# Conversions of the weights w_a and w_b issued behind the gating of the preceding slice, on ACT and on DVE

## Chip, cores, metric

The kernel runs on one core of a Trainium2 chip. The metric is device time in microseconds (us) of one execution; smaller is better. Engines: PE multiplies matrices (PEld is its load of the stationary operand), DVE is the vector engine, ACT the scalar engine, POOL is nearly unused, and SP issues the DMAs. Every engine works through its own instructions in the order in which they were issued to it.

## What is computed

Three stages, each on the output of the one before, on 2304 tokens (4 batches of 512 local and 32 global tokens) of 512 features:

```python
# attention: every local token sees the 32 global keys and a window of 32 keys to either side;
# every global token sees all keys. 8 heads of 64 features.
x = attention(q_l, k_l, v_l, q_g, k_g, v_g)          # (2304, 512)

# first MLP, 512 -> 2048 -> 512
h = x @ w_in
g = np.where(h >= 1, h, np.where(h <= -1, 0.0, (h + 1) ** 2 / 4))
x = g @ w_out

# second MLP, 512 -> 1536 -> 512
a = x @ w_a
b = x @ w_b
out = (a * b) @ w_out2                                # float32
```

The weights arrive as 64-bit floats.

## The kernel before

**Tiles and slices.** The tokens are cut into six tiles (`TILES`, line 43): tiles 0 to 4 have three blocks of 128 tokens, tile 5 one block and the global tokens. The first MLP walks the tiles, and in each tile the 16 slices of 128 hidden features. A pair (t, f) is a unit of the loop at line 728. A unit calls `h_unit(t, f)` (x times w_in, 12 matmuls into a PSUM tile hp), and then `x_unit` of the unit two before (`LAG` at line 727): the gated slice times w_out, 12 matmuls into four PSUM accumulators acc. Every product is three matmuls (`mm3`, lines 423 to 425), since each operand is split into a high and a low part in fp32r.

**The gating** of a slice follows its hp matmuls: ACT takes a relu (line 696), DVE two steps (lines 697 and 698). Its last two instructions, the split of the result g into high and low (ACT line 701, DVE line 702), are put off to the next unit by `flush`.

**Attention** of tile t + 1 runs between the units of tile t (lines 795 to 799). `att_atoms` yields it in pieces per block and pair of heads: load q and k (line 154, two buffers), cast them on ACT (166, 167) and take the rest on DVE (168, 169), score matmuls s (179, 180), masked minimum on DVE (199), exponentials on ACT (203), normalisation (207 to 210), transposes tp on PE (216), copy pt on ACT (220), product with v (226), copy out on DVE (230). The PSUM tiles hp, s, tp and o share four buffers with the tag "h". When a tile begins, its attention output is split into xh on ACT (405) and xl on DVE (406). The global rows, kg and vg (lines 254 and 259), are done in tile 4.

**Conversions.** A weight slice comes as 128 x 512 numbers of 64 bits (`w_load`, one DMA of 512 KB on SP, two raw buffers from tile 1 on). `w_conv` makes 32-bit floats of it: one instruction on ACT, three on DVE:

```python
 97        nc.scalar.activation(tf, f32(high), AF.Copy, scale=W_DOWN)
 98        nc.vector.tensor_scalar(t, t, 3, 0x7FFFFFFF, ALU.logical_shift_left, ALU.bitwise_and)
 99        nc.vector.scalar_tensor_tensor(t, high, -0x80000000, t, ALU.bitwise_and, ALU.bitwise_or)
100        nc.vector.scalar_tensor_tensor(t, low, 29, t, ALU.logical_shift_right, ALU.bitwise_or)
```

In tile 0 the weights of the first MLP are converted as it goes. The 24 slices of w_a and w_b are converted during tiles 1 to 3, ahead of every second unit, and parked in DRAM (wd) until the second MLP loads them again, from the end of tile 4 on:

```python
742                if 1 <= t <= 3 and f % 2 == 0:
743                    i = 8 * (t - 1) + f // 2
744                    if i == 0:
745                        w_load(*ab2[0])
746                    if i + 1 < len(ab2):
747                        w_load(*ab2[i + 1])
748                    (nm, f2), tf = w_conv()
749                    nc.sync.dma_start(wd[f2]["ab".index(nm)], tf)
```

**What sets the order.** The code above is a trace, not the order of issue. A scheduler goes through it with a model of the engines: of the instructions whose operands and buffers are ready it takes the one that was traced first, engine by engine. So an instruction may be issued well ahead of its place in the code, when its engine is idle in the model and it waits for nothing. A conversion needs its raw weights, one of two raw buffers and one of two result buffers, and nothing of the slice at which it stands.

Of the kernel before, what the change touches and what calls it, by code (L numbers as in the profile page):

```python
# [14 lines left out]
AF = mybir.ActivationFunctionType  # L15
ALU = mybir.AluOpType
# [23 lines left out]
W_UP = 256.0  # L40
# [18 lines left out]
def body(tc, qk, qkd, vw, kg, vg, w1i, w1o, w2a, w2b, w2o, mask, out):  # L59
    nc = tc.nc  # L60
# [11 lines left out]
    half = cp.tile([P, 1], F32, name="half")  # L72
# [4 lines left out]
    def f32(t):  # L77
        return t.bitcast(F32)
# [8 lines left out]
    def w_load(key, src):  # L87
        raw = sp["p"].tile([P, 512, 2], I32, name="wraw", bufs=sp["raw"])
        nc.sync.dma_start(raw, src.bitcast(I32).rearrange("p (f two) -> p f two", two=2))
        wq.append((key, raw))  # L90

    def w_conv():
        key, raw = wq.pop(0)
        low, high = raw[:, :, 0], raw[:, :, 1]
        t = sp["p"].tile([P, 512], I32, name="wt", bufs=sp["wt"])
        tf = f32(t)
        nc.scalar.activation(tf, f32(high), AF.Copy, scale=W_DOWN)
        nc.vector.tensor_scalar(t, t, 3, 0x7FFFFFFF, ALU.logical_shift_left, ALU.bitwise_and)
        nc.vector.scalar_tensor_tensor(t, high, -0x80000000, t, ALU.bitwise_and, ALU.bitwise_or)
        nc.vector.scalar_tensor_tensor(t, low, 29, t, ALU.logical_shift_right, ALU.bitwise_or)  # L100
        return key, tf
# [295 lines left out]
    def x_split(t, W):  # L397
        hi, lo = [], []
        last = t == len(TILES) - 1
        for c in range(NC):  # L400
            pool = x5p if last else mp
            h = pool.tile([P, W if last else 384], F32R, name=f"xh{c}", bufs=1)
            l = pool.tile([P, W if last else 384], F32R, name=f"xl{c}", bufs=1)
            src = xraw_cur[t][c]
            nc.scalar.activation(h[:, :W], src[:, :W], AF.Copy)
            nc.vector.tensor_tensor(l[:, :W], src[:, :W], f32(h[:, :W]), ALU.subtract)  # L406
            hi.append(h)
            lo.append(l)
        return hi, lo

    def widths(t):
        return P * len(TILES[t])
# [3 lines left out]
    def flush():  # L416
        d = deferred[:]
        deferred.clear()
        for f in d:
            f()  # L420

    def mm3(acc, whi, wlo, xhi, xlo, first, last):
        nc.tensor.matmul(acc, whi, xhi, start=first, stop=False)  # L423
        nc.tensor.matmul(acc, wlo, xhi, start=False, stop=False)  # L424
        nc.tensor.matmul(acc, whi, xlo, start=False, stop=last)  # L425
# [82 lines left out]
    def ab_load(u):  # L508

        s, f = divmod(u, NF2)  # L510
        for i in range(2):
            t = sp["p"].tile([P, 512], I32, name="wt", bufs=sp["wt"])
            nc.sync.dma_start(f32(t), wd[f][i])
            wt[(u, i)] = f32(t)
# [38 lines left out]
    def raw_to(n):  # L553
        while rawi[0] < min(n, len(ws2)):
            w_load(*ws2[rawi[0]])
            rawi[0] += 1
# [121 lines left out]
    ab2 = [((nm, f2), src[f2]) for f2 in range(NF2) for nm, src in (("a", w2a), ("b", w2b))]  # L678
    ws2 = [(("y", f2), w2o[f2]) for f2 in range(NF2)]

    def h_unit(t, f):
        W = widths(t)
        if t not in xs:
            xs[t] = x_split(t, W)
        hi, lo = xs[t]
        w = wslots[("i", f)]
        hp = ps.tile([P, 512], F32, name="hp", tag="h")
        for c in range(NC):
            s = slice(c * P, (c + 1) * P)
            mm3(hp[:, :W], w[:, 0, s], w[:, 1, s], hi[c][:, :W], lo[c][:, :W], c == 0, c == NC - 1)  # L690
        flush()
        r = mp.tile([P, 384], F32, name="r", tag="r", bufs=3)
        m = mp.tile([P, 384], F32, name="m", bufs=2)
        g = mp.tile([P, 2, 384], F32R, name="g", tag="g", bufs=3)
        gh, gl = g[:, 0], g[:, 1]
        nc.scalar.activation(r[:, :W], hp[:, :W], AF.Relu, bias=half, scale=0.5 / W_UP)  # L696
        nc.vector.scalar_tensor_tensor(m[:, :W], hp[:, :W], 1.0 / W_UP, r[:, :W], ALU.mult, ALU.max)  # L697
        nc.vector.scalar_tensor_tensor(m[:, :W], r[:, :W], 1.0, m[:, :W], ALU.min, ALU.mult)  # L698

        def fin():  # L700
            nc.scalar.activation(gh[:, :W], m[:, :W], AF.Copy)  # L701
            nc.vector.tensor_tensor(gl[:, :W], m[:, :W], f32(gh[:, :W]), ALU.subtract)
        deferred.append(fin)
        gq[(t, f)] = (gh, gl)
# [23 lines left out]
    for u in range(len(units)):  # L728
        for kind in (0, 1):
            if kind == 0:  # L730
                if u >= len(units):
                    continue
                t, f = units[u]
                if t == 0:
                    while W1.si < min(2 * f + LEAD1, len(ws1)):
                        W1.step()
                if t == 1 and f == 0:
                    es_st.close()
                    gp["k"] = es_att.enter_context(tc.tile_pool(name="kp", bufs=1, reuse_waits="tile"))
                    sp["p"] = es_st.enter_context(tc.tile_pool(name="pc", bufs=1, reuse_waits="tile"))  # L740
                    sp["raw"], sp["wt"] = 2, 2
                if 1 <= t <= 3 and f % 2 == 0:
                    i = 8 * (t - 1) + f // 2
                    if i == 0:
                        w_load(*ab2[0])
                    if i + 1 < len(ab2):
                        w_load(*ab2[i + 1])
                    (nm, f2), tf = w_conv()
                    nc.sync.dma_start(wd[f2]["ab".index(nm)], tf)
                if t == len(TILES) - 2 and f == 0:  # L750
                    es_st.close()
                    gp["p"] = es_att.enter_context(tc.tile_pool(name="gp", bufs=1, reuse_waits="tile"))
                if f == 0 and t + 1 < nt:
                    n_items = ends[t + 1] - done["n"]
                    rate = 3.0 * n_items / (2 * (GLOB_END if t == nt - 2 else NF1) - 1)
                    credit = 0.0
                if (t, f) == (nt - 2, GLOB_END):
                    for _ in att:
                        pass
                    es_att.close()  # L760
                    sp["p"] = es_st.enter_context(tc.tile_pool(name="st2", bufs=1, reuse_waits="tile"))
                    sp["raw"], sp["wt"] = RAWBUFS, 4
                    x5p = es_st.enter_context(tc.tile_pool(name="x5p", bufs=1, reuse_waits="tile"))
                    raw_to(RAWBUFS)
                    ab_load(0)
                if t == nt - 1 and f == 0:
                    xs[t] = xs_last
                h_unit(t, f)
                if (t, f) == (nt - 2, GLOB_END + 1):
                    xs_last = x_split(nt - 1, widths(nt - 1))  # L770
                if t == nt - 1:
                    if f == 0:
                        x1_load(0)
                    elif f == 1:
                        ab_sum(0)
                        ab_load(1)
                    elif f in (2, 3):
                        ab_split(0, 2 * f - 4)
                        ab_split(0, 2 * f - 3)
                    elif f == 4:  # L780
                        x_pre(0)
                    if f >= 5 and f < 12:
                        x_op(0, f - 5)
                    elif f == 14:
                        ab_sum(1)
                        ab_split(1, 0)
                    elif f == 15:
                        for part in range(1, 4):
                            ab_split(1, part)
            else:  # L790
                if u < LAG:
                    continue
                tx, fx = units[u - LAG]
                x_unit(tx, fx)
            if u < len(units) and t + 1 < nt:
                credit += rate
                while credit >= 1.0 and done["n"] < ends[t + 1]:
                    credit -= 1.0
                    att_step(ends[t + 1])
        if u < len(units) and f == NF1 - 1 and t + 1 < nt:  # L800
            while att_step(ends[t + 1]):
                pass
# [98 lines left out]
```

## Time and profile before

| | |
|---|---|
| median of 3 runs | 969.54 us (968.93 to 974.25) |
| profiled execution | 972.52 us, of which the span from first to last instruction is 970.7 us |
| busy: PE / PEld / DVE / ACT | 932.9 / 844.5 / 726.7 / 541.6 us |
| moved by DMA | 111.49 MB, 115 GB/s on the mean |

The profile is of one execution. Busy times count an engine's instructions; those of PE overlap, and their ends are modelled. A row of a group names line, engine, operation, output and inputs, then busy time and mean time of one, then the idle time of the engine ahead of these instructions and what ended it. The second MLP begins near 580 us; the first MLP's tiles lie before it.

### The profile page before, as it was taken

Reading aid. Unit: us, or ns where it says so; the run is one execution under the profiler, and the core shown is the slowest. Engines: PE = TensorE matmul, PEld = TensorE weight load, DVE = VectorE, ACT = ScalarE, POOL = GpSimd, SP = SyncE. Lnnn points to the kernel's source line nnn. Section 1 sums busy time; section 2 is a strip of 40 time slices with the busy share of each in tenths; the row PEclk is TensorE's granted clock in tenths of the full one; section 3 lists DMA queues with packets and bytes.
Section 4 is the critical chain, followed back from the end, with each engine's and each line's share of the span. In section 5 each row is a group of like instructions: output and inputs, shape, how many; then the busy total and the mean of one; then the engine's idle time right before and its main releaser. Section 6 shows DMA issues by size and latency. Waiting matters only on the chain.

```text
span 970.7 us, 16708 instructions
## 1 busy us (share of the span) xinstructions
PE 932.9 (96%) x5964; PEld 844.5 (87%) x5964; DVE 726.7 (75%) x1881; ACT 541.6 (56%) x1293; POOL 0.7 (0%) x7
## 2 busy tenths in 40 slices
PE   7899887988999999999999999999999999999997
PEld 5687776978899999998889999999999999999996
DVE  6899999989766666674437978888796666877673
ACT  8867767666555565554445645555554444644441
POOL 0000000000000000000000000000000000000000
PEclk9899998999999999999999999999999999999999
DMA  7455547776622221213536332221241111041101
GB/s 246 147 189 172 177 153 243 243 257 227 213 68 73 65 93 60 79 40 107 156 127 205 93 101 96 87 87 45 64 154 44 51 48 44 32 132 55 55 11 55
DMA packets 55843, 111.49 MB, mean 115 GB/s; under 512 B 6864, under 2 KB 23376, under 8 KB 55760
## 3 DMA queue, kind: packets, MB, share of 16 engines
q1 hardware_dynamic: 55616, 110.26, 35.7%
q8 instruction: 47, 0.77, 0.3%
q14 instruction: 36, 0.29, 0.1%
q10 hardware_dynamic: 144, 0.17, 0.1%
HBM read 95.20 MB, written 15.20 MB: 114 GB/s over the span
## 4 chain that ended last, share of the span: by engine, by line
PE 78%; DVE 10%; DMA 6%; ACT 3%; issue 2%; SPq 0%; ACTq 0%; DVEq 0%
PE hp L423 6%; PE hp L425 5%; PE hp L424 5%; PE acc L423 5%; PE pb L580 5%; PE pb L581 5%; PE py L645 5%; PE pb L578 5%; PE py L646 5%; PE py L644 5%; PE acc L424 5%; PE acc L425 5%; PE px L578 4%; PE px L581 4%; PE px L580 4%; DMA wraw<-in_w2a_dram 3%
## 5 line engine op out<-in xcount | busy, mean ns | idle before, releaser
L423 PE MATMUL hp<-xh,w 128*128 128x384 f32 (+1 forms) x384 | 132.7, 346 | 15.2 <-ACT pt L220 6.8
L423 PE MATMUL acc<-g,w 128*128 128x384 f32 (+1 forms) x384 | 132.7, 346 | 4.3 <-ACT g L701 4.3
L425 PE MATMUL hp<-xl,w 128*128 128x384 f32 (+1 forms) x384 | 127.3, 332 | 0.6 <-DVE xl L406 0.6
L424 PE MATMUL acc<-g,w 128*128 128x384 f32 (+1 forms) x384 | 127.9, 333 | 0.0
L424 PE MATMUL hp<-xh,w 128*128 128x384 f32 (+1 forms) x384 | 126.7, 330 | 0.0
L425 PE MATMUL acc<-g,w 128*128 128x384 f32 (+1 forms) x384 | 125.4, 331 | 0.0
L107 ACT ACTIVATE w<-wt 128x512 fp32r<-128x512 f32 (+1 forms) x116 | 65.0, 564 | 71.0 <-PE pb L581 44.9
L580 PE MATMUL pb<-w 128*128 128x384 f32 (+1 forms) x288 | 94.6, 329 | 0.0
L581 PE MATMUL pb<-w 128*128 128x384 f32 (+1 forms) x288 | 94.3, 327 | 0.0
L423 PEld LDWEIGHTS hp<-xh,w 128*128 128x128 f32 x384 | 73.3, 191 | 23.9 <-ACT pt L220 8.3
L578 PE MATMUL pb<-w 128*128 128x384 f32 (+1 forms) x288 | 93.7, 325 | 0.0
L697 DVE SCALAR_TENSOR_TENSOR m<-hp,r 128x384 f32<-128x384 f32 (+1 forms) x96 | 50.9, 531 | 50.9 <-ACT r L696 50.7
L696 ACT ACTIVATE r<-hp,half 128x384 f32<-128x384 f32 (+1 forms) x96 | 53.6, 558 | 62.5 <-PE hp L425 62.0
L423 PEld LDWEIGHTS acc<-g,w 128*128 128x128 f32 x384 | 72.9, 190 | 12.3 <-ACT g L701 5.8
L645 PE MATMUL py<-w,g 128*128 128x512 f32 x204 | 80.8, 396 | 0.0
L646 PE MATMUL py<-w,g 128*128 128x512 f32 x204 | 80.7, 396 | 0.0
L644 PE MATMUL py<-w,g 128*128 128x512 f32 x204 | 79.6, 390 | 0.0
L701 ACT ACTIVATE g<-m 128x384 fp32r<-128x384 f32 (+1 forms) x96 | 48.4, 504 | 52.8 <-DVE m L698 52.3
L108 DVE TENSOR_TENSOR w<-wsum,w 128x256 fp32r<-128x256 f32 (+1 forms) x108 | 54.6, 507 | 29.8 <-ACT w L107 29.8
L425 PEld LDWEIGHTS hp<-xl,w 128*128 128x128 f32 x384 | 73.3, 191 | 1.8 <-DVE xl L406 1.8
L424 PEld LDWEIGHTS acc<-g,w 128*128 128x128 f32 x384 | 73.1, 190 | 1.6 <-issue 1.0
L425 PEld LDWEIGHTS acc<-g,w 128*128 128x128 f32 x384 | 72.7, 190 | 1.6 <-issue 1.2
(112 smaller groups left out, 2136.2 us busy)
## 6 DMA issues: line engine op xcount, KB each, us to landing
wt<-wd SPq DMA_DIRECT2D x72, 256.0 KB, 2.7
qkd<-in_qkd_dram SPq DMA_DIRECT2D x40, 352.0 KB, 3.2
wraw<-in_w1i_dram SPq DMA_DIRECT2D x16, 512.0 KB, 3.6
wraw<-in_w1o_dram SPq DMA_DIRECT2D x16, 512.0 KB, 4.2
v<-in_vw_dram SPq DMA_DIRECT2D x64, 112.0 KB, 2.6
wraw<-in_w2a_dram SPq DMA_DIRECT2D x12, 512.0 KB, 4.4
wraw<-in_w2b_dram SPq DMA_DIRECT2D x12, 512.0 KB, 4.3
wd<-wt SPq DMA_DIRECT2D x24, 256.0 KB, 2.7
```

Of the source, the lines that this page charges most:

```text
L107: nc.scalar.activation(hi, src, AF.Copy)
L108: nc.vector.tensor_tensor(lo, src, f32(hi), ALU.subtract)
L423: nc.tensor.matmul(acc, whi, xhi, start=first, stop=False)
L424: nc.tensor.matmul(acc, wlo, xhi, start=False, stop=False)
L425: nc.tensor.matmul(acc, whi, xlo, start=False, stop=last)
L578: nc.tensor.matmul(out[:, :n], w[:, 0, r], hi[:, c, :n], start=start and c == 0, stop=False, skip_group_check=True)
L580: nc.tensor.matmul(out[:, :n], w[:, 1, r], hi[:, c, :n], start=False, stop=False, skip_group_check=True)
L581: nc.tensor.matmul(out[:, :n], w[:, 0, r], lo[:, c, :n], start=False, stop=k in (1, 5, 6) and c == 1, skip_group_check=True)
L644: nc.tensor.matmul(a, gh[:, c], w[:, 0], start=f == 0, stop=False)
L645: nc.tensor.matmul(a, gh[:, c], w[:, 1], start=False, stop=False)
L646: nc.tensor.matmul(a, gl[:, c], w[:, 0], start=False, stop=f == NF2 - 1)
L696: nc.scalar.activation(r[:, :W], hp[:, :W], AF.Relu, bias=half, scale=0.5 / W_UP)
```

## The change

A dictionary keeps the last gating instruction of ACT and the last one of DVE that the code has passed. The conversions of w_a and w_b are traced inside `tc.issue_after`, which gives each instruction in the block an edge to the named one on its own engine: it can't be issued before it. The edge is an order of issue alone; no semaphore is added for it. The loads of raw weights and the stores to wd are outside the block.

```diff
+    at = {}
+
+    def paced(fn):
+
+        with tc.issue_after(at["act"]), tc.issue_after(at["dve"]):
+            return fn()
+
     def h_unit(t, f):
...
-        nc.scalar.activation(r[:, :W], hp[:, :W], AF.Relu, bias=half, scale=0.5 / W_UP)
+        at["act"] = nc.scalar.activation(r[:, :W], hp[:, :W], AF.Relu, bias=half, scale=0.5 / W_UP).ins
         nc.vector.scalar_tensor_tensor(m[:, :W], hp[:, :W], 1.0 / W_UP, r[:, :W], ALU.mult, ALU.max)
-        nc.vector.scalar_tensor_tensor(m[:, :W], r[:, :W], 1.0, m[:, :W], ALU.min, ALU.mult)
+        at["dve"] = nc.vector.scalar_tensor_tensor(m[:, :W], r[:, :W], 1.0, m[:, :W], ALU.min, ALU.mult).ins
...
-                    (nm, f2), tf = w_conv()
+                    (nm, f2), tf = paced(w_conv)
                     nc.sync.dma_start(wd[f2]["ab".index(nm)], tf)
```

The order of issue shows what that moves. Lines from 681 on have other numbers after the change: the gating 696 to 698 is 703 to 705, the split 701 and 702 is 708 and 709, and the store 749 is 756.

On DVE, tile 1, the end of the work between the gatings of slices 8 and 9 (raw weights are wraw, a converted slice is wt). Before:

```order
L168 TENSOR_TENSOR qs<-qkd,qs 64x256
L169 TENSOR_TENSOR kl<-qkd,kh 128x448
L207 TENSOR_SCALAR sm<-sm 128x2
L100 SCALAR_TENSOR_TENSOR wt<-wraw,wt 128x512
L208 RECIPROCAL sm<-sm 128x2
L98 TENSOR_SCALAR wt<-wt 128x512
L210 TENSOR_SCALAR e<-e,sm 128x224
L697 SCALAR_TENSOR_TENSOR m<-hp,r 128x384
L99 SCALAR_TENSOR_TENSOR wt<-wraw,wt 128x512
L698 SCALAR_TENSOR_TENSOR m<-r,m 128x384
```

The same stretch after the change:

```order
L168 TENSOR_TENSOR qs<-qkd,qs 64x256
L169 TENSOR_TENSOR kl<-qkd,kh 128x448
L207 TENSOR_SCALAR sm<-sm 128x2
L208 RECIPROCAL sm<-sm 128x2
L210 TENSOR_SCALAR e<-e,sm 128x224
L704 SCALAR_TENSOR_TENSOR m<-hp,r 128x384
L705 SCALAR_TENSOR_TENSOR m<-r,m 128x384
```

Before, conversions stand between nearly all gatings of tile 1 and end in the first slices of tile 2; after the change there is one ahead of every second gating of tiles 1, 2 and 3, and none here.

On DVE, tile 3, ahead of the gating of slice 2. Before:

```order
L168 TENSOR_TENSOR qs<-qkd,qs 64x256
L169 TENSOR_TENSOR kl<-qkd,kh 128x448
L207 TENSOR_SCALAR sm<-sm 128x2
L208 RECIPROCAL sm<-sm 128x2
L210 TENSOR_SCALAR e<-e,sm 128x224
L697 SCALAR_TENSOR_TENSOR m<-hp,r 128x384
L698 SCALAR_TENSOR_TENSOR m<-r,m 128x384
```

After the change:

```order
L168 TENSOR_TENSOR qs<-qkd,qs 64x256
L169 TENSOR_TENSOR kl<-qkd,kh 128x448
L100 SCALAR_TENSOR_TENSOR wt<-wraw,wt 128x512
L207 TENSOR_SCALAR sm<-sm 128x2
L208 RECIPROCAL sm<-sm 128x2
L210 TENSOR_SCALAR e<-e,sm 128x224
L704 SCALAR_TENSOR_TENSOR m<-hp,r 128x384
L705 SCALAR_TENSOR_TENSOR m<-r,m 128x384
```

The other two steps of this conversion, L98 and L99, stand further up in the same slice, to either side of the split of g.

On SP, the last stores to wd and the first load of k for the global rows (kg), which takes space that the conversions leave. Before, in tile 2:

```order
L749 DMA wd_1_108<-wt 128x512
L89 DMA wraw<-in_w2b_dram 128x1024
L749 DMA wd_0_109<-wt 128x512
L749 DMA wd_1_110<-wt 128x512
L154 DMA qkd<-in_qkd_dram 128x704
L254 DMA kg<-in_kg_dram 128x576 x2
```

After the change, at the end of tile 3:

```order
L756 DMA wd_0_109<-wt 128x512
L154 DMA qkd<-in_qkd_dram 128x704
L173 DMA v<-in_vw_dram 112x256
L756 DMA wd_1_110<-wt 128x512
L173 DMA v<-in_vw_dram 112x256
L254 DMA kg<-in_kg_dram 128x576 x2
L259 DMA vg<-in_vg_dram 128x640 x2
```

The stores of two conversions are now two slices apart, with loads of the attention between them, and the load of kg has moved behind the last of them.

## Rows read from the trace of the kernel before

**Rows 1.** The page: busy time, share of the span and instructions of each engine.

```profile
PE 932.9 (96%) x5964; PEld 844.5 (87%) x5964; DVE 726.7 (75%) x1881; ACT 541.6 (56%) x1293; POOL 0.7 (0%) x7
```

**Rows 2.** Stretches, each engine's busy time (instructions), clock, DMA share: tiles 1, 2, 3.

```profile
138.40:247.00 108.60, 95.92 (x594) 86.70 (x593) 98.32 (x273) 73.13 (x181) 0.00 (x0) 0.97 0.75 241
247.00:338.10 91.10, 89.39 (x577) 83.05 (x577) 63.18 (x185) 54.75 (x140) 0.00 (x0) 0.98 0.32 101
338.10:425.10 87.00, 87.00 (x578) 81.69 (x577) 58.50 (x176) 51.69 (x134) 0.00 (x0) 1.00 0.22 68
```

**Rows 3.** Costliest groups, 138 to 255 us.

```profile
L423 PE MATMUL hp<-xh,w 128*128 128x384 f32 x68 | 24.6, 362 | 9.9 <-ACT pt L220 5.8 <-DVE m L697 3.0 <-ACT xh L405 1.1
...
L99 DVE SCALAR_TENSOR_TENSOR wt<-wraw,wt 128x512 int32<-128x512 int32 x24 | 16.5, 687 | 0.1
L97 ACT ACTIVATE wt<-wraw 128x512 f32<-128x512 f32 x24 | 16.0, 667 | 17.1 <-DMA wraw<-in_w2a_dram 11.4 <-DMA wraw<-in_w2b_dram 5.6
...
L98 DVE TENSOR_SCALAR wt<-wt 128x512 int32<-128x512 int32 x24 | 10.1, 422 | 7.9 <-ACT wt L97 7.9
```

**Rows 4.** Stretch of tile 1, DVE's instructions of line 98 alone.

```profile
138.40:247.00 108.60, 9.28 (x22) 0.97 0.75 241
```

**Rows 5.** Costliest groups, 256 to 425 us.

```profile
L423 PE MATMUL hp<-xh,w 128*128 128x384 f32 x124 | 43.5, 351 | 0.0
```

**Rows 6.** Timeline: start, duration, engine, instruction, wait; starts of tiles 1 and 2.

```profile
143.97 0.67 ACT L97 ACTIVATE wt<-wraw 128x512 f32<-128x512 f32 x1 [2.69 <-DMA wraw<-in_w2b_dram]
...
144.67 0.43 DVE L98 TENSOR_SCALAR wt<-wt 128x512 int32<-128x512 int32 x1 [1.24 <-ACT wt L97]
145.01 0.69 DVE L100 SCALAR_TENSOR_TENSOR wt<-wraw,wt 128x512 int32<-128x512 int32 x1
145.62 0.55 DVE L697 SCALAR_TENSOR_TENSOR m<-hp,r 128x384 f32<-128x384 f32 x1
...
146.77 0.34 PE L179 MATMUL s<-kh,qs 128*128 128x224 f32 x1 [1.48 <-DVE qs L168]
...
249.27 0.44 PE L423 MATMUL hp<-xh,w 128*128 128x384 f32 x1 [1.08 <-ACT xh L405]
```

**Rows 7.** Stretches as in rows 2: start, body of tile 1, start of 2; tile 3.

```profile
138.40:159.30 20.90, 17.17 (x86) 14.63 (x85) 19.20 (x54) 14.72 (x38) 0.00 (x0) 0.92 0.79 249
159.30:247.00 87.70, 78.75 (x511) 72.06 (x510) 79.12 (x221) 58.40 (x143) 0.00 (x0) 0.98 0.74 239
247.00:256.20 9.20, 7.49 (x34) 6.41 (x33) 7.45 (x19) 5.05 (x11) 0.00 (x0) 0.81 0.36 142
338.10:343.10 5.00, 5.00 (x34) 4.96 (x33) 2.80 (x10) 2.24 (x6) 0.00 (x0) 1.00 0.01 2
343.10:348.60 5.50, 5.50 (x39) 5.08 (x37) 4.31 (x12) 3.24 (x10) 0.00 (x0) 1.00 0.37 113
348.60:425.10 76.50, 76.50 (x510) 71.65 (x509) 51.39 (x156) 46.22 (x121) 0.00 (x0) 1.00 0.22 69
```

**Rows 8.** A stretch at the start of tile 2, columns as in rows 2.

```profile
251.70:255.00 3.30, 3.30 (x13) 3.30 (x12) 3.30 (x8) 1.76 (x4) 0.00 (x0) 0.50 0.21 79
```

**Rows 9.** Timeline, gatings of slices 2 and 3 of tile 3.

```profile
351.06 0.34 DVE L210 TENSOR_SCALAR e<-e,sm 128x224 f32<-128x224 f32 x1
352.10 0.56 DVE L697 SCALAR_TENSOR_TENSOR m<-hp,r 128x384 f32<-128x384 f32 x1 [0.71 <-ACT r L696]
...
353.91 0.44 PE L423 MATMUL hp<-xh,w 128*128 128x384 f32 x1
...
356.92 0.56 DVE L697 SCALAR_TENSOR_TENSOR m<-hp,r 128x384 f32<-128x384 f32 x1 [2.32 <-ACT r L696]
```

**Rows 10.** The page: DMA issues, xcount, KB each, us to landing.

```profile
wd<-wt SPq DMA_DIRECT2D x24, 256.0 KB, 2.7
```

**Rows 11.** Instructions of the tile kg: duration min/median/max, first and last start; landing.

```profile
L267 PE MATMUL sg<-kg x128: 389/389/413, 435.2 to 488.6; 64*32 64x272 f32 x128
...
DMA to landing us min/median/max: 2.8/3.2/4.7
```

## The prediction, made before the change was run

> **What bounds the kernel now.** I read the page first: PE is busy for 932.9 us of a span of 970.7 [rows 1], so nearly everything that can be won is time in which PE does less than it could. To find that time I cut the span into the tiles of the first MLP, each from its first hp matmul to the next tile's first one, and asked for the busy time of each engine in each stretch. Tile 1 lasts 108.6 us, tile 2 91.1 and tile 3 87.0 [rows 2], although tile 3 holds nearly the same PE work: 578 PE instructions against 594 in tile 1 and 577 in tile 2. In tile 3 PE is busy without a gap and DVE for 58.50 us; in tile 1 DVE is busy for 98.32 of 108.60 us, and the granted clock is 0.97. So two stretches with the same work run under two bounds: tile 3 under PE, tile 1 under DVE.
>
> What makes DVE so much longer in tile 1 is in the costliest groups of the stretch 138 to 255 us: all 24 conversions of w_a and w_b are there (L98 and L99, 24 of each, 422 and 687 ns, and L100, which has the form and length of L99), though the loop traces one conversion for every two slices of tiles 1 to 3, which is 8 for each tile [rows 3]; 22 of them start inside tile 1 [rows 4]. They ran ahead, because the order of issue let them in as soon as their buffers were free. The cost on PE is in the first rows of that view: the hp matmuls of L423 waited 9.9 us, for a PSUM copy on ACT (5.8) and for the gating on DVE (3.0). In the stretch 256 to 425 us, after the last conversion, the same group shows no wait at all [rows 5].
>
> **What a conversion weighs.** Its three DVE instructions last 0.42, 0.69 and 0.69 us by the mean of their groups, 1.80 us [rows 3]. Back to back they take less of DVE, since the next one starts before the record of the last one ends: an L98 at 144.67, an L100 at 145.01 and the next instruction at 145.62 [rows 6] give steps of 0.34 and 0.61 us; with L99, which has the length of L100, 0.34 + 0.61 + 0.61 = 1.56 us. ACT's part (L97) is 0.67 us. Each also has a load of 512 KB and a store of 256 KB on SP. 22 of the 24 fall into tile 1 now and 8 will; 14 leave, which is 14 x 1.56 = 22 us of DVE. 98.3 less 22 leaves some 76 us of DVE for a tile whose PE work needs about 89 (87.0 x 594 / 578), so DVE is no longer the bound there. For tile 3 the same sum gives 58.5 + 8 x 1.56 = 71.0 us of 87.0, also below PE.
>
> **Term 1, the body of tile 1 (159.3 to 247.0 us).** It holds 511 PE instructions in 87.7 us; the body of tile 3 holds 510 in 76.5 [rows 7]. With DVE relieved it should run at tile 3's rate: 87.7 - 76.5 = 11.2 us gained. The bounds are 0, if something other than DVE sets this pace, and 11.2. I take all of it, because in tile 3 the same chain of attention, gating and matmuls shows what the pace is with no conversions, and the cost of those that stay has a term of its own.
>
> **Term 2, the start of tile 1 (138.4 to 159.3 us).** 86 PE instructions take 20.9 us; at the rate of the start of tile 3 (73 in 5.0 + 5.5 = 10.5 us [rows 7]) they would take 12.4, so 8.5 us is the ceiling and 0 the floor. Only part of it is the conversions'. ACT stood for 2.69 us at 143.97 until the raw weights of the second conversion landed, with the gating and the casts of q and k queued behind; DVE waited 1.24 us for ACT at 144.67 in the same way, and PE then waited 1.48 us for the first score matmul [rows 6]. That conversion now stands two slices later, and of four conversions in the stretch one stays: 3 x 1.56 = 4.7 us of DVE go. But the loads for the first scores still queue on SP behind two loads of raw weights, as before, and the attention of the next tile still has to start from nothing. I take 3.0 us, near the 2.69 us of the one wait that I can name.
>
> **Term 3, the start of tile 2 (247.0 to 256.2 us).** 34 PE instructions take 9.2 us where the start of tile 3 needs 5.0 for 34 [rows 7]. [...] 4.2 us gained, between 0 and 4.2; with tile 1 on time nothing else holds the split back.
>
> **Term 4, what the 16 conversions cost in tiles 2 and 3.** Their cover is DVE's idle time, and what they can hit is the gating, which frees the PSUM buffer that a later hp matmul writes. The tightest place that I find is slice 2 of tile 3: DVE ends its softmax part at 351.40, idles for 0.71 us, and the gating runs from 352.10 to 352.66; the next hp matmul starts at 353.91 [rows 9]. So a conversion in this gap (1.56 us against 0.71 idle) makes the gating 0.85 us late, and PE still has 1.25 us before it would wait. Floor 0. As a ceiling every one of the 16 loses the 0.85 us, 13.6 us. I take 0.5 us, near the floor, because PE shows no wait in the same tiles and ahead of the next gating DVE idles for 2.32 us [rows 9], so that the lag is made good there. The loads are spread as well: tile 3 has DMA at 0.22 of its engines' time now, against 0.75 in tile 1 [rows 2].
>
> One thing of the move is on SP. The first load of k for the global rows takes the space that the conversions leave, and is now queued behind their last store. The last conversion belongs to slice 14 of 16 of tile 3, near 338.1 + 14 x 87.0 / 16 = 414.2 us, and ends within a slice of that; with 2.7 us for the store [rows 10] the load can start near 420. It lands after 3.2 us (4.7 at most), and its first matmul is at 435.2 [rows 11], so some 10 us of cover are left: nothing. The tiles after that keep their order on PE and DVE, and nothing is counted for them.
>
> **Sum.** 11.2 + 3.0 + 4.2 - 0.5 = 17.9 us. The profiled execution took 972.52 us (span 970.7, 1.8 us around it), 3.0 above the median of the runs; taken off the median, 969.54 - 17.9 = **951.6 us**.
>
> A check by PE's own rows: the matmul rows leave 12.7 us idle in tile 1 and 1.7 in tile 2, 14.4 us in all, and this view alone would give 955.1. [...]
>
> **Rivals.**
> - *Half of it* (0.16). Tile 1's pace is set by its own attention chain and not by DVE. For it: the largest wait of hp is for a copy on ACT (5.8 of 9.9), and PE's order in tile 1 has the transposes right behind each hp group. Against it: ACT is busy for 73.13 of 108.60 us there [rows 2], and its queue was held by loads of raw weights for 17.1 us [rows 3], which goes. Then term 1 is 5.6, term 2 nothing: 5.6 + 4.2 - 0.5 = 9.3, so 960.2 us.
> - *Given back* (0.05). The stalls move along with the conversions: 16 of them at the 0.85 us of the tight slice take 13.6 of 18.4, which leaves 5 or less, 965 to 970 us. Against it are the 1.25 us of slack. That the order does not do what it says belongs here; the rows of the order show the conversions at one for two slices, so I give it next to nothing.
> - *Slower* (0.04). A conversion at the head of DVE waits for ACT or for its load, and the gating, the softmax and the split of g behind it wait too; PE loses the whole 1.80 us at each of the 16: 28.8 - 18.4 = 10.4 us more, 980 us. It decides the sign from 18.4 / 16 = 1.15 us of lost PE time for each conversion. The 1.24 us of the conversion at 144.67 show such a wait [rows 6]. [...] Against it: L97 is now issued right behind the gating's first step on ACT, and its raw weights are loaded two slices ahead.
>
> **How the numbers follow.** The forecast has 0.75. Its own ends are the full 8.5 of term 2 with no cost (23.9 us gained, 945.6) and term 2 at nothing with some 1.5 of cost (14, 955.6). The range reaches on to the first rival, 945.6 to 961.0, and leaves out the other two, about 0.1. What a measurement of this kernel can tell from no change is 0.5%, 4.8 us, so faster means below 964.7: 0.91 by the forecast and the first rival, same 0.05, slower 0.04.
>
> **What would show it.** Right: tile 1 at 92 to 97 us, tiles 2 and 3 both at 87 to 88, with L98 to L100 eight times in each; DVE at about 0.8 in all three; the hp group of L423 with less than 3 us of waits between tile 1 and tile 4; one stretch at half clock at the start of tile 1 and none later. Wrong: tile 3 longer than 89 us with waits for L697 (term 4), tile 1 above 100 us with ACT or loads as what is waited for (terms 1 and 2), or the global rows starting late behind the load of k.

## The result, and the profile after

| | before | after |
|---|---|---|
| median of the runs beside each other | 969.77 us (4 runs, 968.93 to 974.25) | 956.43 us (4 runs, 954.88 to 960.08) |
| profiled execution | 972.52 us | 954.88 us |
| ratio | | 0.985, 95% interval 0.9826 to 0.9874 |

The change makes the kernel faster by 1.5% (1.3 to 1.7). The two profiled executions differ by 17.6 us, where the prediction had 17.9; the medians differ by 13.3.

The page of the changed kernel, its busy times and its slices for PE, DVE and the granted clock:

```profile
PE 926.9 (97%) x5964; PEld 840.3 (88%) x5964; DVE 728.2 (76%) x1881; ACT 539.6 (57%) x1293; POOL 0.7 (0%) x7
...
PE   7898988999999999999999999999999999999997
...
DVE  6799999888877877764348968888896666877663
...
PEclk9899999999999999999999999999999999999999
```

The work is the same as in rows 1 (1881 instructions on DVE, 1293 on ACT), PE idles less, and DVE's digits are 7 and 8 from 167 to 405 us, a stretch over which they fell from 9 to 6 before. The stretches of tiles 1, 2 and 3 of the changed kernel, columns as in rows 2:

```profile
138.10:233.80 95.70, 92.67 (x594) 83.83 (x592) 80.98 (x234) 65.70 (x171) 0.00 (x0) 1.00 0.52 166
233.80:320.70 86.90, 86.90 (x577) 81.59 (x577) 70.25 (x199) 56.00 (x142) 0.00 (x0) 1.00 0.46 148
320.70:407.90 87.20, 87.20 (x579) 81.78 (x578) 70.17 (x199) 56.17 (x143) 0.00 (x0) 1.00 0.44 142
```

Against rows 2, tile 1 went from 108.6 to 95.7 us and tile 2 from 91.1 to 86.9; tile 3 took on eight conversions (DVE from 58.50 to 70.17 us) and is 87.2 instead of 87.0. The granted clock is 1.00 in all three. The same in finer pieces (start and body of tile 1, start of tile 2), to set beside rows 7:

```profile
138.10:155.90 17.80, 15.02 (x78) 12.11 (x76) 16.13 (x44) 11.82 (x32) 0.00 (x0) 1.00 0.71 228
155.90:233.80 77.90, 77.65 (x519) 71.72 (x517) 64.85 (x191) 53.88 (x140) 0.00 (x0) 1.00 0.48 152
233.80:243.00 9.20, 9.20 (x61) 8.74 (x61) 7.50 (x21) 5.36 (x14) 0.00 (x0) 1.00 0.43 128
```

And the costliest groups of tiles 1 to 3, for the waits of rows 3:

```profile
L423 PE MATMUL hp<-xh,w 128*128 128x384 f32 x204 | 71.4, 350 | 0.3 <-ACT pt L220 0.2
...
L97 ACT ACTIVATE wt<-wraw 128x512 f32<-128x512 f32 x24 | 16.0, 666 | 0.0
```

The hp matmuls waited 9.9 us and now wait 0.3. The cast on ACT, L97, had 17.1 us of idle time ahead of it, until its raw weights landed; now it has none. That second row is the one on which the reading of this result turns.

### The profile page after: what moved, and what is told of

Same layout as the page of the kernel before. It is cut to its first block, busy times and chain, and to the rows that moved or that the text cites. A ratio compares the mean times of both kernels' runs of the same rounds, so it can differ in the third digit from the quotient of the medians.

```text
span 953.1 us, 16713 instructions
## 1 busy us (share of the span) xinstructions
PE 926.9 (97%) x5964; PEld 840.3 (88%) x5964; DVE 728.2 (76%) x1881; ACT 539.6 (57%) x1293; POOL 0.7 (0%) x7
## 4 chain that ended last, share of the span: by engine, by line
PE 84%; DVE 9%; ACT 3%; DMA 2%; issue 1%; SPq 0%; ACTq 0%; DVEq 0%
PE hp L423 6%; PE hp L425 6%; PE hp L424 6%; PE acc L423 6%; PE acc L424 5%; PE acc L425 5%; PE pb L580 5%; PE pb L581 5%; PE py L645 5%; PE pb L578 5%; PE py L646 5%; PE py L644 5%; PE px L578 4%; PE px L581 4%; PE px L580 4%; PE o L226 3%
## 5 line engine op out<-in xcount | busy, mean ns | idle before, releaser
L423 PE MATMUL hp<-xh,w 128*128 128x384 f32 (+1 forms) x384 | 131.5, 342 | 5.4 <-ACT xh L405 2.1
L423 PE MATMUL acc<-g,w 128*128 128x384 f32 (+1 forms) x384 | 132.0, 344 | 4.2 <-ACT g L708 3.6
L107 ACT ACTIVATE w<-wt 128x512 fp32r<-128x512 f32 (+1 forms) x116 | 64.9, 564 | 70.8 <-PE pb L581 44.9
L578 PE MATMUL pb<-w 128*128 128x384 f32 (+1 forms) x288 | 93.7, 325 | 0.0
L423 PEld LDWEIGHTS hp<-xh,w 128*128 128x128 f32 x384 | 72.9, 190 | 12.8 <-issue 3.4
L423 PEld LDWEIGHTS acc<-g,w 128*128 128x128 f32 x384 | 72.4, 189 | 12.5 <-issue 5.3
```

The costliest lines, as they stand in the source:

```text
L107: nc.scalar.activation(hi, src, AF.Copy)
L578: nc.tensor.matmul(out[:, :n], w[:, 0, r], hi[:, c, :n], start=start and c == 0, stop=False, skip_group_check=True)
```

## The experiments

My theory going in was the prediction's: DVE's load made tile 1 long, and spreading it relieves PE. The rivals were ACT, whose queue stood still until raw weights had landed, and the traffic of 768 KB for each conversion. Here is all that ran, with the lengths of the tiles in each one's profile; the runs follow one by one. "Ahead" means without an edge, "behind" with one; "by data" that the instructions follow ACT's, since L98 reads what L97 wrote. The kernel before had medians of 971.79, 971.16 and 972.29 us in the three batches (e1 to e4; e6, e7, e9; e8, e10 and the repetitions).

| kernel | ACT's cast | DVE's steps | tile 1 | tile 2 | tile 3 | median, us |
|---|---|---|---|---|---|---|
| before | ahead | ahead | 108.6 | 91.1 | 87.0 | 969.77 |
| e4_no_dve | ahead | none | 105.8 | 86.9 | 87.0 | 966.58 |
| e10_loads | none | none | 96.1 | 86.9 | 87.0 | 957.73 |
| e8_paced_no_dve | behind | none | 93.7 | 86.9 | 87.0 | 956.17 |
| after | behind | behind | 95.7 | 86.9 | 87.2 | 956.43 |
| e2_act_edge | behind | by data | 95.7 | 86.9 | 87.6 | 956.36 |
| e3_dve_edge | ahead | behind | 96.6 | 92.1 | 92.2 | 965.90 |
| e6_twice | behind | behind, reckoned 2.78 us each | 97.1 | 87.0 | 88.4 | 957.73 |
| e6_thrice | behind | behind, reckoned 4.0 us each | 104.0 | 94.9 | 95.1 | 980.85 |
| e9_dense | behind, at every slice | behind, at every slice | 100.2 | 90.3 | 87.0 | 961.52 |
| e7_odd | behind, odd slices | behind, odd slices | 93.9 | 87.0 | 87.0 | 953.59 |

**The changed kernel again (e1_repeat, and e1_again in a later batch).** No edit.

> The changed kernel as it is, once more, with a profile of its own. If the lengths of the tiles make the whole difference, every execution has tile 1 at 95 to 97 us and tiles 2 and 3 at 87, and the time is 953 to 957 us, 14 to 17 below the kernel before. If what separates its executions lies elsewhere, the tiles stay and another stretch, or the clock, differs between the two profiles by 2 us or more.

> The changed kernel, for that comparison: 954 to 958 us, tile 1 near 95.7.

Measured: 956.56 us against 971.79 before (ratio 0.985, 0.9813 to 0.9886), and 955.66 against 972.29 (0.9835, 0.9798 to 0.9872). The tiles of the later profile, whose execution was among the fastest:

```profile
136.30:232.80 96.50, 92.94 (x595) 83.99 (x594) 81.01 (x234) 65.86 (x171) 0.00 (x0) 1.00 0.52 166
232.80:319.70 86.90, 86.90 (x577) 81.59 (x576) 70.25 (x199) 56.07 (x143) 0.00 (x0) 1.00 0.47 148
319.70:406.80 87.10, 87.10 (x578) 81.69 (x577) 70.06 (x199) 56.11 (x143) 0.00 (x0) 1.00 0.45 142
```

In e1_repeat tile 1 was 95.6 us long:

```profile
138.00:233.60 95.60, 92.67 (x593) 83.80 (x593) 80.93 (x234) 65.72 (x171) 0.00 (x0) 1.00 0.53 168
```

The tiles of the three profiles hold within 1 us, the time of the executions doesn't: 954.56 to 962.22 us in the later batch. All three profiles are of executions under 956 us, so where the longer ones lose their time no profile shows; the last section has the granted clock that goes with it.

**One edge alone (e2_act_edge, e3_dve_edge).**

```diff
-        with tc.issue_after(at["act"]), tc.issue_after(at["dve"]):
+        with tc.issue_after(at["act"]):
```

That is e2_act_edge; e3_dve_edge has `at["dve"]` alone in this line.

> Only the edge on ACT is kept. L98 on DVE reads what L97 wrote, so my theory (only the place of the conversions counts, and the data give it to DVE too) expects the same time as with both edges within 2 us, 953 to 958. If the edge on DVE carries the gain, by what it is that DVE issues first, 960 us or more.

> Only the edge on DVE is kept; ACT may cast as far ahead as its two result buffers go. My theory (DVE's share is what bound tile 1) expects 954 to 959 us: all of the gain but for ACT's wait for the raw weights at the start of tile 1 (2.7 us), which comes back. If the waits at the head of ACT were the cause, most of the gain goes: 963 us or more.

Measured: ACT's edge alone gives all of it, 956.36 us (ratio 0.9848, 0.9812 to 0.9883), as expected. Its tile 1:

```profile
138.90:234.60 95.70, 92.75 (x595) 83.89 (x594) 80.89 (x235) 66.01 (x171) 0.00 (x0) 1.00 0.54 167
```

DVE's edge alone gives less than two fifths, 965.90 us (0.9943, 0.9918 to 0.9969), outside what I expected and on the rival's side. DVE's steps stand behind the same gatings as after the change; tile 1 of this kernel is short, and tiles 2 and 3 lose 5 us each:

```profile
139.80:236.40 96.60, 93.24 (x594) 83.95 (x593) 79.10 (x230) 65.54 (x170) 0.00 (x0) 1.00 0.53 166
236.40:328.50 92.10, 89.03 (x577) 83.01 (x576) 68.47 (x195) 54.22 (x140) 0.00 (x0) 0.98 0.43 135
328.50:420.70 92.20, 88.67 (x577) 81.73 (x578) 72.45 (x205) 57.53 (x147) 0.00 (x0) 1.00 0.44 139
```

DVE is busy for 68 to 72 us there, where after the change it is 70. What is new stands in the groups of tiles 2 and 3 (236.4 to 420.7 us):

```profile
L423 PE MATMUL hp<-xh,w 128*128 128x384 f32 x129 | 46.0, 356 | 4.8 <-DVE m L704 2.2 <-ACT pt L220 1.7 <-ACT xh L405 0.9
...
L97 ACT ACTIVATE wt<-wraw 128x512 f32<-128x512 f32 x14 | 9.3, 664 | 20.4 <-DMA wraw<-in_w2b_dram 14.1 <-DMA wraw<-in_w2a_dram 6.1
```

ACT stood for 20.4 us ahead of 14 casts, 20.2 of them until raw weights had landed; in tile 1 of this kernel, with 10 casts, it was 4.0 us. One of these waits, from the timeline of the same kernel (start, duration, instruction, wait):

```profile
258.47 0.66 ACT L97 ACTIVATE wt<-wraw 128x512 f32<-128x512 f32 x1 [4.16 <-DMA wraw<-in_w2b_dram]
259.63 0.56 DVE L704 SCALAR_TENSOR_TENSOR m<-hp,r 128x384 f32<-128x384 f32 x1 [4.53 <-ACT r L703]
...
260.24 0.44 PE L423 MATMUL hp<-xh,w 128*128 128x384 f32 x1 [2.15 <-DVE m L704]
```

A cast issued too early reaches the head of ACT's queue 4.16 us before its weights are there. Behind it waits the gating's relu, so DVE waits 4.53 us for it with nothing wrong on its own side, and PE waits 2.15 us for the buffer that the gating frees. This chain needs no load on DVE at all. Half clock follows:

```profile
261.30:264.70 3.40, 3.40 (x14) 3.40 (x13) 3.34 (x10) 1.28 (x5) 0.00 (x0) 0.51 0.30 75
```

This run also gives a price for the waits by themselves. Tiles 2 and 3 hold 14 casts here and 15 after the change, with DVE's work within 1 us, and are 184.3 us long instead of 174.1: 10.2 us for 20.2 us of waits, half a microsecond for each microsecond.

**DVE's steps taken out, without edges (e4_no_dve) and with both (e8_paced_no_dve).**

```diff
+    def w_conv_act():
+        key, raw = wq.pop(0)
+        t = sp["p"].tile([P, 512], I32, name="wt", bufs=sp["wt"])
+        tf = f32(t)
+        nc.scalar.activation(tf, f32(raw[:, :, 1]), AF.Copy, scale=W_DOWN)
+        return key, tf
...
-                    (nm, f2), tf = w_conv()
+                    (nm, f2), tf = w_conv_act()
```

In e8_paced_no_dve the call is `paced(w_conv_act)`.

> The kernel before, without edges, and the 24 conversions of w_a and w_b leave out their three DVE instructions (ACT's cast, the loads and the stores stay, so the weights of the second MLP are not what they should be). If DVE's load made tile 1 long, tile 1 falls to 90 to 97 us though everything else runs ahead as before, and the time is 951 to 958 us. If the attention chain, ACT's waits for raw weights or the loads themselves set the pace, tile 1 stays over 101 us and the time over 962.

> The changed kernel with both edges, and the conversions without their three DVE instructions (so the weights of the second MLP are not what they should be). Beside the same omission without edges, which had tile 1 at 105.8 us, it changes only where ACT's casts and their loads and stores stand. If casts that run ahead of their loads and wait at the head of ACT are enough to make tile 1 long, tile 1 is at 93 to 96 us here, tiles 2 and 3 at 87, the time 953 to 957. If something else of the conversions than their place does it, tile 1 stays over 101.

Measured: without edges 966.58 us (0.9946, 0.9922 to 0.997), with them 956.17 (0.9817, 0.9776 to 0.9858). The first went against my theory. Its tile 1:

```profile
136.40:242.20 105.80, 96.15 (x594) 86.34 (x593) 69.45 (x210) 74.38 (x186) 0.00 (x0) 0.97 0.82 272
```

and in its groups of that tile (the numbers of lines are larger by 7 here: L107 is the cast, L430 the hp matmul, L227 the copy of tp):

```profile
L430 PE MATMUL hp<-xh,w 128*128 128x384 f32 x64 | 23.3, 364 | 5.0 <-DVE m L704 2.6 <-ACT pt L227 2.4
...
L107 ACT ACTIVATE wt<-wraw 128x512 f32<-128x512 f32 x24 | 16.0, 666 | 18.5 <-DMA wraw<-in_w2a_dram 9.3 <-DMA wraw<-in_w2b_dram 8.3 <-ACT e L210 0.9
```

DVE fell from 98.32 to 69.45 us of work and tile 1 only from 108.6 to 105.8. ACT still stood for 18.5 us, 17.6 of them until raw weights had landed. The twin with edges:

```profile
140.00:233.70 93.70, 91.40 (x594) 83.59 (x593) 69.54 (x210) 66.44 (x171) 0.00 (x0) 1.00 0.55 171
```

Same work on DVE (69.54 us), and 12.1 us less. So the place of the casts, with their loads and stores and the half clock (0.97 against 1.00), is worth 12.1 us of tile 1 with DVE busy for some 69.5 us in both; DVE's steps are worth 2.8 us when casts run ahead (108.6 less 105.8) and 2.0 when they don't (95.7 less 93.7).

**Loads and stores alone, running ahead (e10_loads).** POOL, which has nothing else to do, takes the place of ACT and DVE:

```diff
+    def w_conv_pool():
+        key, raw = wq.pop(0)
+        t = sp["p"].tile([P, 512], F32, name="wt", bufs=sp["wt"])
+        nc.gpsimd.memset(t, 0.0)
+        nc.gpsimd.tensor_copy(t[:, 0:1], f32(raw)[:, 0, 1:2])
+        return key, t
...
-                    (nm, f2), tf = w_conv()
+                    (nm, f2), tf = w_conv_pool()
```

> The kernel before, without edges, and the conversions of w_a and w_b without ACT and DVE: POOL clears the result tile and copies one column of the raw weights, so that the loads and stores run ahead as before (the weights of the second MLP are zero but for that column). If the traffic itself, 768 KB for each conversion packed into tile 1, delays the attention's loads, tile 1 is over 101 us. If waits at the heads of ACT and DVE and their work do it, tile 1 is at 90 to 96 us, and the time is 950 to 957.

Measured: 957.73 us (0.9839, 0.9796 to 0.9883), tile 1 at 96.1 us:

```profile
139.50:235.60 96.10, 92.69 (x595) 85.05 (x594) 70.00 (x209) 61.31 (x162) 18.48 (x46) 0.98 0.89 299
```

All the traffic is packed into tile 1, at 299 GB/s with the DMA engines busy for 0.89, more than in any other kernel here, and the tile is 2.4 us longer than with paced conversions and no DVE steps (93.7). So the traffic by itself is not what made 108.6. Between this run and e4_no_dve lie the casts on ACT: 9.7 us. How much of that is the wait ahead of a cast and how much the 0.57 us or so that the cast itself takes on ACT (in the kernel before one starts at 163.41 and the relu behind it at 163.98) isn't separated by a run in this tile; ACT was busy for 74.38 of 105.8 us, so it was not full. An estimate by the price that e3_dve_edge gave makes the 17.6 us of waits in e4_no_dve worth some 9 us, most of the 9.7; e9_dense below shows that casts which hardly wait aren't free either.

**More work on DVE, at the changed places (e6_twice, e6_thrice).** L99 and L100 are repeated, which changes nothing in what they write (e6_thrice has `range(3)`):

```diff
-        nc.vector.scalar_tensor_tensor(t, high, -0x80000000, t, ALU.bitwise_and, ALU.bitwise_or)
-        nc.vector.scalar_tensor_tensor(t, low, 29, t, ALU.logical_shift_right, ALU.bitwise_or)
+        for _ in range(2):
+            nc.vector.scalar_tensor_tensor(t, high, -0x80000000, t, ALU.bitwise_and, ALU.bitwise_or)
+            nc.vector.scalar_tensor_tensor(t, low, 29, t, ALU.logical_shift_right, ALU.bitwise_or)
```

> The changed kernel, with L99 and L100 of each paced conversion issued a second time (they change nothing when repeated): 2.78 us of DVE for each instead of 1.56, at the same places. Term 4 of the prediction saw 1.25 us between the gating and the next hp matmul at the tightest slice, of which a conversion uses some; with 1.22 us more I expect PE to lose up to 1 us in one or two slices of each tile: tiles 2 and 3 at 88 to 89, the time 956 to 960 us. If conversions in tiles 2 and 3 are as costly as the rival 'given back' has it, 1 us or more at each of 16, 970 us or more.

> The same with L99 and L100 three times: 4.0 us of DVE for each conversion, 8 in a tile, so that DVE has about as much to do in tile 1 (60 + 32 = 92 us) as in the kernel before (98), with no cast of ACT that runs ahead of its load. If DVE's load made tile 1 of the kernel before long, tile 1 comes to 103 us or more here. If ACT's waits for raw weights at the head of its queue did (new theory, after two runs went against the first), tile 1 is at 96 to 100 us, and tiles 2 and 3 at 88 to 93, what DVE's load of about 90 us gives.

Measured: twice gives 957.73 us (0.9859, 0.9832 to 0.9886), thrice 980.85 (1.0113, 1.0075 to 1.015), slower than before the change. By DVE's busy time in tile 2 (78.43 and 87.83 us, against 58.35 in e8_paced_no_dve) a conversion took 2.5 and 3.7 us of DVE, less than the 2.78 and 4.0 that I had reckoned. Twice came out near what I expected, tile 2 better:

```profile
137.40:234.50 97.10, 93.48 (x594) 85.50 (x593) 89.05 (x249) 65.63 (x171) 0.00 (x0) 0.98 0.51 165
234.50:321.50 87.00, 87.00 (x579) 81.70 (x578) 78.43 (x213) 54.43 (x140) 0.00 (x0) 1.00 0.47 145
321.50:409.90 88.40, 87.25 (x578) 81.69 (x578) 79.27 (x215) 55.55 (x144) 0.00 (x0) 1.00 0.46 143
```

Against the changed kernel the three tiles are 1.4, 0.1 and 1.2 us longer, so the cover of term 4 was real and has room. Thrice:

```profile
138.30:242.30 104.00, 95.88 (x595) 86.88 (x594) 96.63 (x262) 63.39 (x168) 0.00 (x0) 0.97 0.47 149
242.30:337.20 94.90, 90.21 (x577) 83.32 (x576) 87.83 (x229) 54.89 (x142) 0.00 (x0) 0.98 0.43 135
337.20:432.30 95.10, 90.71 (x579) 83.34 (x578) 88.12 (x232) 55.48 (x143) 0.00 (x0) 0.98 0.40 126
```

This went against the new theory in its plain form, which had 96 to 100 for tile 1. With casts that never wait for their weights, a DVE that is busy for 96.63 us goes with a tile 1 of 104.0 us, and 88 us of DVE make a tile of 87 us one of 95. So DVE's load does cost: with DVE at 90% of a tile (e6_twice, tiles 2 and 3) 0.1 and 1.2 us, at 93% (here) 8. The lumps grew together with the load, so which of the two costs isn't shown. In the kernel before both faults lay in the same tile, each by itself was enough for a tile of 104 us or more (DVE's load in the longer lumps of this run), and they don't add up: without DVE's steps 2.8 us go, and with DVE paced but not the casts (e3_dve_edge) tile 1 is short and the loss is in tiles 2 and 3.

**A conversion at every slice (e9_dense).**

```diff
-                if 1 <= t <= 3 and f % 2 == 0:
-                    i = 8 * (t - 1) + f // 2
+                if 0 <= 16 * (t - 1) + f < len(ab2):
+                    i = 16 * (t - 1) + f
```

> The changed kernel with a conversion at every slice of tile 1 and of the first half of tile 2, all behind the gating of the slice before on both engines. DVE then has 60 + 16 x 1.56 = 85 us of work in tile 1. If the waits of ACT for its loads are what cost, tile 1 stays at 96 to 99 us, tile 2 at 87 to 89, tile 3 at 87, and the time is 955 to 961 us, with ACT's waits for raw weights under 4 us. If DVE's load near that of PE is what costs, tile 1 is over 101 us and the time over 962.

Measured: 961.52 us (0.9911, 0.9879 to 0.9944). Tile 1 came to 100.2 us, between the two expectations, and the profile is of the slowest of its executions (966.95 us). Tile by tile it still tells something. Tiles 1 and 2, and L97 in each of them:

```profile
141.60:241.80 100.20, 94.13 (x594) 85.39 (x593) 89.64 (x252) 68.50 (x177) 0.00 (x0) 0.98 0.67 214
241.80:332.10 90.30, 88.36 (x577) 81.64 (x576) 72.80 (x205) 57.08 (x146) 0.00 (x0) 1.00 0.50 154
```

```profile
L97 ACT ACTIVATE wt<-wraw 128x512 f32<-128x512 f32 x16 | 10.7, 668 | 0.9 <-DMA wraw<-in_w2a_dram 0.9
```

```profile
L97 ACT ACTIVATE wt<-wraw 128x512 f32<-128x512 f32 x8 | 5.3, 668 | 4.5 <-DMA wraw<-in_w2a_dram 3.1 <-DMA wraw<-in_w2b_dram 1.3
```

In tile 1 ACT hardly waits. Beside tile 1 of e6_twice, with as much work on DVE (89.05 us), it is 3.1 us longer, with 16 casts instead of 9 and more traffic (214 GB/s instead of 165): the two together cost something almost without a wait, and which of them does isn't told apart. In tile 2 DVE has 72.80 us of work and ACT waits 4.4 us for its weights; that tile is 3.4 us longer than after the change.

**Conversions at the odd slices (e7_odd, e7_odd_again).**

```diff
-                if 1 <= t <= 3 and f % 2 == 0:
+                if 1 <= t <= 3 and f % 2 == 1:
```

> The changed kernel with the conversions at the odd slices: the first two loads of raw weights then stand behind the first two loads of q and k on SP, not ahead of them. The first scores of tile 1 can start some 1 to 2 us sooner, so tile 1 at 93 to 95 and the time 1 to 2 us under the changed kernel, 953 to 956. If the start of tile 1 is bound by the attention chain itself, no difference.

> The conversions at the odd slices once more, beside the changed kernel in the same batch: 1 to 4 us below it if the first result holds, tile 1 near 94 us.

Measured: 953.59 us (0.9816, 0.9792 to 0.9841), and 953.21 (0.98, 0.9768 to 0.9832) beside the changed kernel's 955.66 in the same batch. Tile 1 of the first:

```profile
137.60:231.50 93.90, 91.22 (x594) 83.53 (x593) 79.90 (x234) 65.92 (x170) 0.00 (x0) 1.00 0.52 166
```

The first score matmul of tile 1 starts 4.9 us into the tile and not 7.0, from the timelines of this kernel and of the changed one:

```profile
142.48 0.27 PE L179 MATMUL s<-kh,qs 128*128 128x224 f32 x1
```

```profile
145.06 0.34 PE L179 MATMUL s<-kh,qs 128*128 128x224 f32 x1
```

This version is faster than the kernel before. Against the changed kernel the intervals of the two ratios overlap (0.9832 against 0.9798), so the 2.4 us between the medians alone don't show it to be faster; that tile 1 is shorter, the profiles do show, with 93.9 and 94.0 us in two against 95.7, 95.6 and 96.5 in three.

## Why the prediction was right, and where it was not

**Direction and size.** Faster was given 0.91, and the measured 956.43 us lies in the range and under 964.7. Between the profiled executions the sum is out by 0.3 us of 17.9, and tile by tile it holds: tile 1 at 95.7 (said: 92 to 97), tiles 2 and 3 at 86.9 and 87.2 (87 to 88), DVE at 0.80 to 0.85 of the three, less than 3 us of waits at L423 (0.3). One stretch at half clock was said for the start of tile 1, and there is none.

**Terms.** The pieces must be compared with care, since 8 of PE's instructions moved from the start of tile 1 to its body; at 76.5 / 510 = 0.15 us each that is 1.2 us. Term 1, 11.2 us: the body went from 87.7 to 77.9, 9.8, or 11.0 with the moved work. Term 2, 3.0: the start went from 20.9 to 17.8, 3.1, of which 1.2 is that work, so 1.9. Term 3, 4.2: tile 2 is shorter by 4.2, all of it. Term 4, 0.5: 0.2 in tile 3. Together that is 16.9; the other 0.7 us between the profiles lie outside the three tiles. Wrong in size was what a conversion weighs on DVE: the prediction had 1.56 us, and so 76 us of work for tile 1; by the tiles without these steps it was (98.32 - 69.54) / 22 = 1.31 us in the kernel before, and tile 1 came to 80.98. The value of no term rests on it; the ceiling of term 4 does. The load of k behind the last store cost nothing: its first matmul is again 10 us into tile 4 (418.0 after 407.9; before, 435.2 after 425.1).

**The level.** Taken off the median, 951.6 us was 4.8 too low, and that is not in the terms: the profiled execution of before was 3.0 above the median of the three runs that I had, the one of after 1.6 below its own. In the later batches the kernel before had medians of 971 to 972, above the 969.5 that I started from; there the change is worth 15.2 (971.79 less 956.56) and 16.6 us (972.29 less 955.66).

**The step that failed** is the one in the first paragraph: "So two stretches with the same work run under two bounds: tile 3 under PE, tile 1 under DVE." That DVE was busy for 98.32 of 108.60 us was no proof of it. The prediction's own sum had DVE with 76 us of work after the change and 98 before, and a tile of 108.6 us leaves DVE idle for 10; the kernel without DVE's steps showed 105.8, with DVE at 69.45. So the casts that ran ahead on ACT were enough to hold tile 1 without DVE's load. By e6_thrice (104.0) a DVE as busy as that can hold it too, at least in longer lumps; how the two shared the tile in the kernel before is not shown. The row that points to the casts was in the prediction, L97 with 17.1 us of waits for its raw weights [rows 3], and I used it as a point against the first rival. In term 2 I named one of these waits (2.69 us) and priced it, and did not ask for the other eleven. The same wait, further into tile 1 of the kernel before, from its timeline:

```profile
163.41 0.66 ACT L97 ACTIVATE wt<-wraw 128x512 f32<-128x512 f32 x1 [0.67 <-DMA wraw<-in_w2a_dram]
163.98 0.57 ACT L696 ACTIVATE r<-hp,half 128x384 f32<-128x384 f32 x1
...
164.44 0.59 ACT L220 ACTIVATE pt<-tp 112x512 f32<-112x512 f32 x1
...
165.09 0.44 PE L423 MATMUL hp<-xh,w 128*128 128x384 f32 x1 [1.51 <-ACT pt L220]
```

ACT waits 0.67 us for the weights, then does the cast, the relu and the copy in this order, and PE waits 1.51 us for the copy. The view of waits puts that down to "ACT pt", which is why the largest wait of hp (5.8 of 9.9) looked like the attention's own chain. The sum came out right all the same, because its terms were taken from lengths of tiles and not from DVE's load, and because the edge on ACT moves the casts away as well. That was luck: for DVE's edge alone the same theory gave 954 to 959 us, and 965.90 was measured.

**The check by PE's rows.** Tiles 1 and 2 became 17.1 us shorter (12.9 and 4.2). The idle time of the matmul rows had given 14.4, so more was won than these rows showed as idle. Of what they leave out, some 5.0 us are the three stretches at half clock in these tiles (3.4, 3.3 and 3.3 us at a granted clock of 0.50), through which PE counts as busy; this is an estimate, half of their length. Nor did the largest share of busy time tell what to relieve first: in tile 1 DVE had it (98.32 of 108.60 us, PE 95.92), and without DVE's steps the tile lost 2.8 us, with the edge on ACT alone 12.9.

**The rivals.** "Half of it" had the right engine and the wrong conclusion: ACT's queue was enough to set the pace, but by casts that the change moves too. "Given back" was answered by e6_twice: with L99 and L100 twice, tiles 2 and 3 were 0.1 and 1.2 us longer. "Slower" described a mechanism that exists, an instruction at the head of a queue that is waiting for its load; e3_dve_edge shows it on ACT at 4.16 us, with a stretch at half clock shortly behind it (0.51 for 3.40 us). After the change it doesn't occur: L97 waits 0.0 us for its weights.

## What to carry to other kernels

A share of busy time near 90% is a reason to look, not a bound (here DVE's 98.32 of 108.60 us, and 2.8 us less of tile 1 without its steps): take the suspect's work out, and see whether the stretch gets shorter. Where two faults lie in one stretch, either can be enough, so taking one out shows little; put the suspect's work alone in as well, as e6_thrice does. Where one engine's queue serves both the critical path and a stream that waits for DMA, look at the idle time ahead of that stream's instructions, released by DMA: here it delayed whatever was queued behind (a cast that stood for 4.16 us on ACT, and DVE 4.53 us for the relu behind it, in e3_dve_edge), and the waits then appeared under the names of the instructions behind. If a stream is to be paced, pace its first instruction, the one that touches the loaded data; here that edge alone gave the whole gain (956.36 us), and the edge on the later engine less than two fifths of it (965.90).

## What the runs showed that I had not expected

**Executions of one kernel differ, and the granted clock with them.** In the last batch the changed kernel took 954.56 us at a mean granted clock of 0.997 and 962.22 at 0.989, 7.7 us for 0.008; and 0.008 of 957 us is 7.7. What lowered the clock in the longer execution is not shown. In the profile of the kernel before (clock 0.990), half clock shows once at the start of tile 2 [rows 8] and twice in tile 1:

```profile
149.30:152.70 3.40, 3.40 (x12) 2.96 (x13) 3.34 (x12) 2.59 (x8) 0.00 (x0) 0.50 0.83 236
166.40:169.70 3.30, 3.30 (x17) 2.85 (x17) 3.24 (x11) 2.50 (x8) 0.00 (x0) 0.50 0.50 168
```

Each time PE had waited shortly before: 1.48 us until 146.77 and 1.51 until 165.09 in tile 1, 1.08 until 249.27 in tile 2. After the change tiles 1 to 3 had none, though PE was still idle for 2.8 of the first 17.8 us of tile 1; so not every wait is followed by one. Those that were cost their own length and, by an estimate from the two levels of the clock (1.00 and 0.50), half of the stretch at 0.50 behind them. By a second estimate, some 5 to 6 us of what separates the two profiles are the clock's: 0.990 to 0.996 of some 960 us is 5.8.

**Traffic was cheaper than waits.** With 299 GB/s through it, tile 1 was 2.4 us longer than with 171 GB/s and nine casts on ACT (e10_loads, e8_paced_no_dve), while 24 casts ahead on ACT made it 9.7 us longer than e10_loads.
